# Products of ones into bank 0 where the planned order leaves TensorE without filler, in a recurrent-attention and mixture-of-experts kernel

## Chip, cores and metric

One core of one Trainium2 chip. The metric is device microseconds of one execution; the figure for a kernel is the median of its runs. The profile is one further execution under the hardware profiler.

## What is computed

Three stages. The first is a recurrence over 768 time steps with a 40 x 40 state for each of 4 x 8 heads; the second weighs eight experts with a gate that is normalized over rows and columns in turn; the third is one wide layer with an ELU.

```
for t in range(S):                              # S = 768, D = 40, 32 heads
    y[:, :, t] = einsum('bhd,bhde->bhe', rt, state)
    Sa = einsum('bhde,bhe->bhd', state, at)
    state = state * wt[:, :, None, :] - outer(Sa, bt) + outer(vt, kt)
x = y as [3072, 320]
P = exp(x @ w_gate - max); eight times: rows, then columns normalized
out = sum over e of P[:, e] * (relu(x @ w1[e]) @ w2[e])      # 8 experts, F = 1024
result = elu(out @ w_in) @ w_out                              # width 2048
```

## The kernel before, in words

**Stages.** The recurrence is turned into block algebra over 12 chunks of 64 steps. One chunk takes, in this order: loads (`load_in`, `load_r`, `load_v`); a scan of the decays and reciprocals (`scan`, `recip0` to `recip2`) on VectorE and ScalarE; products of BK with AW (`gmm`, L672, four groups), transposes of AW and BK (`at_t`, `kb_t`); a trip of l_d through DRAM; an elimination of 31 steps on VectorE (`t_mul`, `t_add`, L720 to L730, on TMP and U); a trip of u_d through DRAM; small 32 x 32 products (`emm`, `t21`) and `pmm` (TT with GS, L774); and then, for four groups in a row, the serial part in which the state is carried on (`rvmm`, `y0mm`, `qsmm`, `ysmm`, `trmm`; their results are masked into RHS, and into STMP, ST and Y, by VectorE). `y_out`, `x_in` and `xsplit` turn a chunk's output into the operand XS of the experts; `gatemm` makes its logits.

**Fillers.** Experts 0 and 1 work on a chunk as soon as its XS is there. Their products (XS with w, 128 x 128 x 256; hh or hl with w, 128 x 128 x 320) are cut into short items (`moe0_items`, L878; `moe1_items`, L906), which the planner puts wherever TensorE would else be free. Fillers use banks 0 to 3; attention uses banks 4 to 7. Expert 1 has only the first NSTR = 4 of its 8 blocks done here, and only for chunks 0 to 9; its weights pass through a ring, and a weight split (`stream_split`: a ScalarE copy, a GpSimd subtraction and the reload of the staging tile on SP) is an item of its own. For chunk 9 three more weight splits close the list. Items start in their order: each waits for the first step of the one before (L193 to L198).

**The order.** `Order` (L52) records every call of the first stage as tasks with steps, each on one engine, prices each step (`price`, L130), links steps that touch the same data (`link`, L167), and then plays the engines through by those prices (`run`, L209): of the steps that are ready it takes the one that could begin first, within 200 ns the one of the highest rank, and fillers rank lowest. A spare bank is handed out as it comes free. The planned sequence is then issued to the engines (`replay`, L303); every engine works its own queue in that order. The planner ends when all attention steps are placed; fillers that are left, and chunk 11's, follow in a loop (`moe0_rest`, L1070), in which the gate's normalization is interleaved. After that come all six token blocks for the rest of expert 1, experts 2 to 7 and the last layer (`p2_m1`, `p2_m2`, L1152 to L1184), with TensorE work back to back.

A matmul with both operands in fp32 is recorded as two instructions, one with fp32r operands as one. So the 32 products of one chunk's BK with AW are 64 records, and eight of TT with GS are 16.

Of the kernel before, what the change touches and what calls it, by code (L numbers as in the profile page):

```python
# [9 lines left out]
F32 = mybir.dt.float32  # L10
F32R = mybir.dt.float32r
# [4 lines left out]
ALU = mybir.AluOpType  # L16
# [4 lines left out]
NE, NSETS, NF = 8, 10, 8  # L21
# [1 line left out]
NC = S // C  # L23
NG = 4
NSLOT = 11
NSTR = 4
BIG_X = float(2.0**40)
BIG_W = float(2.0**56)
TINY = float(2.0**-60)
# [16 lines left out]

class Task:
    def __init__(self, f, args, rank=0.0):
        self.f, self.args, self.steps, self.bank, self.rank = f, args, [], None, rank


class Order:  # L52
# [34 lines left out]
    def add(self, f, *args):  # L87
        t = Task(f, args, 1e3 * AHEAD.get(f.__name__, 0))
        self.record(t)
        if t.steps:  # L90
            self.tasks.append(t)
        return bool(t.steps)

    def region(self, ap):

# [113 lines left out]
    def run(self, until=None):  # L209

        self.until = until
        self.link()
        free = dict.fromkeys(("PE", "V", "A", "P", "SP"), 0.0)
        transfers = 0.0
        banks = [0.0] * len(self.banks)
        ready = {e: [] for e in free}
        owed = sum(s.task.f is not until for s in self.steps)

        def open_(s):
            s.left = -1  # L220
            ready[s.eng].append(s)

        for s in self.steps:
            s.left, s.at = len(s.before), 0.0
        for s in self.steps:
            if s.left == 0:
                open_(s)

        def may(s):
            if not s.task.banked or s.task.bank is not None:  # L230
                return True
            return all(p.left == -2 or p.task is s.task for x in s.task.steps for p in x.before)

        done, mode = [], None

        def worth(s):
            return s.rank + (1e3 * self.SAME if s.eng == "PE" and self.tiles(s) == mode else 0.0)

        while owed:
            best = None  # L240
            for e, waiting in ready.items():
                for s in waiting:
                    at = max(free[e], s.at)
                    if e == "SP":
                        at = max(at, transfers - self.QUEUE)
                    if s.task.banked and s.task.bank is None:
                        if not may(s):
                            continue
                        at = max(at, min(banks))
                    key = (at, -s.rank)  # L250
                    if best is None or key < best[0]:
                        best = (key, s)
            at, s = best[0][0], best[1]

            for x in ready[s.eng]:
                begin = max(free[s.eng], x.at)
                if x.eng == "SP":
                    begin = max(begin, transfers - self.QUEUE)
                if x.task.banked and x.task.bank is None:
                    if not may(x):  # L260
                        continue
                    begin = max(begin, min(banks))
                if begin <= at + self.SLACK and worth(x) > worth(s):
                    s = x
            begin = max(free[s.eng], s.at, transfers - self.QUEUE if s.eng == "SP" else 0)
            if s.task.banked and s.task.bank is None:
                b = min(range(len(banks)), key=lambda i: banks[i])
                begin = max(begin, banks[b])
                banks[b] = 1e12
                old = s.task.steps  # L270
                s.task.bank = b
                self.record(s.task)
                for x, y in zip(old, s.task.steps):
                    x.calls = y.calls
                s.task.steps = old
            ready[s.eng].remove(s)
            end = begin + s.cost
            if s.eng == "PE":
                m = self.tiles(s)
                end += 110 * (mode is not None and m != mode)  # L280
                mode = m
            free[s.eng] = end
            result = end + s.tail
            if s.eng == "SP":
                move = s.tail - self.DMA
                transfers = max(transfers, end) + move
                result = transfers + self.DMA
            s.left, s.begin = -2, begin
            done.append(s)
            owed -= s.task.f is not until  # L290
            if s.task.banked and s is s.task.steps[-1]:
                banks[s.task.bank] = result
            for n in s.after:
                n.left -= 1
                n.at = max(n.at, end + 20 * (s.eng != "PE") if n.eng == s.eng != "SP" else result + 40)
                if n.left == 0:
                    open_(n)
        self.done = done
        begun = {s.task for s in done}
        self.replay(done + [s for t in self.tasks for s in t.steps if t in begun and s.left != -2])  # L300
        return [t for t in self.tasks if t not in begun]
# [4 lines left out]
                getattr(self.engines[s.eng], method)(*args, **kwargs)  # L306

    SLACK, QUEUE, FILL, FED, SAME = 200.0, 1000.0, 0.0, 2000.0, 0.0

    @staticmethod  # L310
    def tiles(s):
# [176 lines left out]
def kernel(  # L488
# [64 lines left out]
        wload(i + len(wst))  # L553

    def stream_load(k):
        if k < 10 * NSTR:
            SP.dma_start(out=wst[k % 2], in_=wslab[NF + k % NSTR])

    def stream_split(k):
        if k < 10 * NSTR:
            st, w = wst[k % 2], wring[NF + k % 3]
            A.copy(out=w[:, 0, :], in_=st)
            P.tensor_tensor(out=w[:, 1, :], in0=st, in1=fv(w[:, 0, :]), op=ALU.subtract)
            stream_load(k + 2)
# [339 lines left out]
    def moe1_items(c):  # L906
        x = XS[c % 2]
        if c == 0:
            for k in range(2):
                stream_load(k)  # L910
            for k in range(3):
                stream_split(k)
                yield
        for f in range(NSTR + 1):
            k = c * NSTR + f
            if f < NSTR:
                for half in range(2):
                    mm1(bank[f % 2][:, 0:256], wring[NF + k % 3], x, 4 * half, 4 * half + 4)
                    if half == 1:
                        relu_split(bank[f % 2][:, 0:256], hh[f % 2][:, 0:256], hl[f % 2][:, 0:256])  # L920
                    yield
            if f > 0:
                for t in range(2):
                    cs = slice(128 * t, 128 * t + 128)
                    mm2(bank[2 + t][:, 0:320], hh[(f - 1) % 2][:, cs], hl[(f - 1) % 2][:, cs], wring[NF + (k - 1) % 3],
                        f == 1, f == NSTR)
                    if t == 1 and f == NSTR:
                        for tt in range(2):
                            A.copy(out=YE[:, tt, :], in_=bank[2 + tt][:, 0:320])
                        SP.dma_start(out=ye_d[1][2 * c:2 * c + 2].rearrange("n p d -> p n d"), in_=YE)  # L930
                    yield
                if k + 2 < 10 * NSTR:
                    stream_split(k + 2)
                    yield
        if c == 9:
            wlimit[0] = NSETS * NF - 1
            wload(NF + 1)
            for n in range(NF, NSLOT):
                wsplit(n)
                yield  # L940
# [9 lines left out]
    for c in range(NC):  # L950
# [33 lines left out]
            order.add(f, c)  # L984
        if c < NC - 1:
            stream = chain(moe0_items(c), moe1_items(c) if c < 10 else ())
            while order.add(item):
                pass

    manual = ctx.enter_context(ExitStack())  # L990
    manual.enter_context(tc.manual_schedule())
# [18 lines left out]
    P.memset(Y, 0.0)  # L1010
    V.memset(bank[4], 0.0)

    left = order.run(item)
    ph1.close()

# [5 lines left out]
    OUT = [p2.tile([128, 4, 320], F32, name=f"OUT{j}") for j in range(6)]  # L1021
    RAW = p2.tile([128, 352, 2], I32, name="RAW")
    EX = [p2.tile([128, 512], F32, name=f"EX{i}") for i in range(2)]
    NX = [p2.tile([128, 512], F32, name=f"NSTR{i}") for i in range(2)]
    GX = [p2.tile([128, 512], F32, name=f"GX{i}") for i in range(2)]

    hookq = deque()
# [78 lines left out]
    def evac(s, j):  # L1106
        for t in range(4):
            ps, o, n = bank[2 + t][:, 0:320], OUT[j][:, t, :], 4 * j + t
            if s == 1:
                V.tensor_scalar(out=o, in0=ps, scalar1=pp[:, n, 1:2], scalar2=None, op0=ALU.mult)  # L1110
            elif s < 8:
                V.scalar_tensor_tensor(out=o, in0=ps, scalar=pp[:, n, s:s + 1], in1=o, op0=ALU.mult, op1=ALU.add)  # L1112
            elif s == 8:
# [31 lines left out]

        return [c0, c1]

    first = lambda s, j: NSTR if s == 1 and j < 5 else 0
    units = [(1, j, f) for j in FIRST for f in range(first(1, j), NF)]
    units += [(s, j, f) for s in range(2, NSETS) for j in range(6) for f in range(NF)]  # L1150

# [19 lines left out]
    def p2_m2(i):  # L1171
# [6 lines left out]
        if f == 7:  # L1178
            evac(s, j)
            if s == 7:  # L1180
                for kt in range(3):
                    hookq.append((10, lambda kt=kt: xt2(j, kt)))
        if j == (4 if s == 1 and f >= NSTR else 5):
            late.append(lambda: post_m2(s, f))  # L1184

    LAG = 3
# [102 lines left out]
```

## Time and profile before

| | us |
|---|---|
| median of 3 runs | 2342.08 |
| lowest and highest run | 2340.38, 2345.02 |
| the profiled execution | 2344.47 |
| its span, first to last instruction | 2342.8 |
| outside the span | 1.7 |
| TensorE busy | 2217.4 (95%) |
| VectorE busy | 1235.3 (53%) |
| ScalarE busy | 900.8 (38%) |
| mean granted TensorE clock | 0.953 |

TensorE's clock is granted at one of two levels, 2.4 GHz (1.00) or 1.2 GHz (0.50); a value between is a mean over a stretch. Idle time of an engine is put down to what ended it. Time under "busy" of TensorE is that of modelled, pipelined matmuls: at half clock the same work shows as more busy time.

### The profile page before, as it was taken

The numbers are of one execution on the slowest core, as the hardware profiler recorded it, in microseconds if no ns is written. First come the engines' busy times: TensorE is split into PE (matmuls) and PEld (weight loads), VectorE is DVE, ScalarE is ACT, GpSimd is POOL, SyncE is SP. The second block draws the span as 40 slices with busy tenths as digits, with TensorE's granted clock in tenths as the row PEclk, the third lists the DMA queues.
The fourth block names the chain that finished last, engine by engine and source line by source line (L and its number), as shares of the span: only waits on it lengthen the run. The fifth ranks groups of instructions, "written<-read, shape, count | busy, mean of one in ns | idle before, by whom it ended". The sixth has DMA issues, their size and how long they took to land.

```text
span 2342.8 us, 41612 instructions
## 1 busy us (share of the span) xinstructions
PE 2217.4 (95%) x17276; PEld 1999.4 (85%) x17276; DVE 1235.3 (53%) x2494; ACT 900.8 (38%) x1865; POOL 306.1 (13%) x319
## 2 busy tenths in 40 slices
PE   3888899999999899999999999999999999999997
PEld 3777788888888889999999999999999998999996
DVE  7775478777776363555555442222222333556664
ACT  3454455555555321112112112112112224777664
POOL 2121222222221220002002002002002002001000
PEclk9776899989999899999999999999999999999998
DMA  3443444444443360213222101001001001000000
GB/s 99 100 120 89 107 127 118 134 118 125 113 117 109 98 192 19 78 60 97 76 65 78 48 23 50 1 1 50 1 1 50 1 1 50 1 1 20 19 24 28
DMA packets 171397, 152.60 MB, mean 65 GB/s; under 512 B 107648, under 2 KB 142336, under 8 KB 170240
## 3 DMA queue, kind: packets, MB, share of 16 engines
q1 hardware_dynamic: 171200, 149.86, 23.0%
q8 instruction: 138, 2.26, 0.4%
q14 instruction: 59, 0.48, 0.1%
HBM read 114.83 MB, written 35.00 MB: 64 GB/s over the span
## 4 chain that ended last, share of the span: by engine, by line
PE 86%; DVE 9%; issue 2%; ACT 1%; DMA 1%; SPq 0%; POOL 0%; DVEq 0%; ACTq 0%
PE bank L573 32%; PE bank L306 23%; PE bank L583 10%; PE bank L582 10%; PE bank L581 10%; DVE TMP L306 2%; DVE U L306 2%; DVE RHS L306 1%; DMA wst<-in_wslab_dram 1%; DVE STMP L306 0%; DVE Y L306 0%; DVE ST L306 0%; PE bank L1098 0%; SPq L306 0%; ACT GS L306 0%
## 5 line engine op out<-in xcount | busy, mean ns | idle before, releaser
L573 PE MATMUL bank<-X,w 128*128 128x512 f32 x3296 | 827.6, 392 | 0.0
L573 PEld LDWEIGHTS bank<-X,w 128*128 128x128 f32 x3296 | 601.1, 188 | 105.5
L577 DVE SCALAR_TENSOR_TENSOR hl<-bank,hh 128x512 fp32r<-128x512 f32 x320 | 220.4, 690 | 606.9 <-ACT hh L576 606.9
L583 PE MATMUL bank<-w,hl 128*128 128x320 f32 x1664 | 514.9, 309 | 0.3 <-DVE hl L1092 0.3
L582 PE MATMUL bank<-w,hh 128*128 128x320 f32 x1664 | 514.3, 309 | 0.0
L581 PE MATMUL bank<-w,hh 128*128 128x320 f32 x1664 | 513.7, 309 | 0.0
L576 ACT ACTIVATE hh<-bank 128x512 fp32r<-128x512 f32 x320 | 191.7, 599 | 813.7 <-PE bank L573 812.1
L581 PEld LDWEIGHTS bank<-w,hh 128*128 128x128 f32 x1664 | 313.2, 188 | 16.0
L582 PEld LDWEIGHTS bank<-w,hh 128*128 128x128 f32 x1664 | 313.1, 188 | 15.9
L583 PEld LDWEIGHTS bank<-w,hl 128*128 128x128 f32 x1664 | 313.0, 188 | 0.5 <-DVE hl L1092 0.5
L552 POOL TENSOR_TENSOR w<-wst,w 128x704 fp32r<-128x704 f32 x69 | 118.5, 1719 | 1245.2 <-ACT w L551 1234.0
L306 PE MATMUL bank<-XS,w 128*128 128x256 f32 x1024 | 161.7, 306 | 0.0
L306 PEld LDWEIGHTS bank<-XS,w 128*128 128x128 f32 x1024 | 142.8, 207 | 6.7 <-issue 3.3
L306 DVE TENSOR_TENSOR TMP<-U,LD 128x126 f32<-128x126 f32 (+22 forms) x372 | 135.0, 363 | 13.3 <-DMA LD<-l_d 1.9
L325 DVE SCALAR_TENSOR_TENSOR NSTR<-EX,NSTR 128x512 f32<-128x512 f32 x96 | 67.4, 702 | 135.5 <-ACT NSTR L324 135.2
L306 PE MATMUL bank<-w,hh 128*128 128x320 f32 x512 | 129.5, 340 | 0.1
L306 DVE TENSOR_TENSOR U<-U,TMP 128x126 f32<-128x126 f32 (+22 forms) x372 | 110.4, 297 | 11.4
L1112 DVE SCALAR_TENSOR_TENSOR OUT<-bank,pp,OUT 128x320 f32<-128x320 f32 x144 | 69.3, 544 | 54.1 <-PE bank L583 54.1
L306 POOL TENSOR_TENSOR w<-wst,w 128x704 fp32r<-128x704 f32 x43 | 73.9, 1722 | 175.5 <-ACT w L306 95.0
L306 PE MATMUL bank<-BK,AW 40*64 40x128 f32 x768 | 63.3, 333 | 32.0 <-issue 24.7
L306 DVE SCALAR_TENSOR_TENSOR hl<-bank,hh 128x512 fp32r<-128x512 f32 (+1 forms) x84 | 47.1, 561 | 87.0 <-ACT hh L306 86.6
L306 PEld LDWEIGHTS bank<-w,hh 128*128 128x128 f32 x512 | 87.5, 201 | 4.9 <-issue 1.9
(133 smaller groups left out, 2444.7 us busy)
## 6 DMA issues: line engine op xcount, KB each, us to landing
wst<-in_wslab_dram SPq DMA_DIRECT2D x104, 352.0 KB
RAW<-in_wslab_dram SPq DMA_DIRECT2D x32, 352.0 KB
BK<-in_wakb_dram SPq DMA_DIRECT2D x24, 320.0 KB
x_d<-XS SPq DMA_DIRECT2D x12, 640.0 KB
X<-x_d SPq DMA_DIRECT2D x12, 640.0 KB
ye_d<-YE SPq DMA_DIRECT2D x22, 320.0 KB
XS<-ye_d SPq DMA_DIRECT2D x11, 640.0 KB
LD<-l_d SPq DMA_DIRECT2D x24, 256.0 KB
```

Of the source, the lines that this page charges most:

```text
L306: getattr(self.engines[s.eng], method)(*args, **kwargs)
L325: nc.vector.scalar_tensor_tensor(out=n, in0=e, scalar=1.0, in1=n, op0=ALU.add, op1=ALU.mult)
L552: (V if i < NF else P).tensor_tensor(out=w[:, 1, :], in0=st, in1=fv(w[:, 0, :]), op=ALU.subtract)
L573: PE.matmul(ps, w[:, pl, c0:c0 + 128], x[:, m, :], start=(t == 0), stop=(t == 7))
L576: A.activation(out=h_hi, in_=ps, func=AF.Relu)
L577: V.scalar_tensor_tensor(out=h_lo, in0=ps, scalar=0.0, in1=fv(h_hi), op0=ALU.max, op1=ALU.subtract)
L581: PE.matmul(acc, h_hi, hi, start=first, stop=False)
L582: PE.matmul(acc, h_hi, lo, start=False, stop=False)
L583: PE.matmul(acc, h_lo, hi, start=False, stop=last)
L1112: V.scalar_tensor_tensor(out=o, in0=ps, scalar=pp[:, n, s:s + 1], in1=o, op0=ALU.mult, op1=ALU.add)
```

## The change

The planner keeps a running account of how much of TensorE's array the planned products have used in the last 3.4 us of planned time (`heat`, `activity`). When a TensorE step is placed and would leave TensorE free before it, and no started filler has unplanned steps, and the next filler in line is the first of a chunk (`head`) or there is none, then products of the constant `ones` with itself into bank 0, columns 0 to 127, are put in front of it, at 220 ns each, as long as the account stands below 2600. The count of blocks of expert 1 becomes a list per token block, and three places follow that list. One tile gets another name.

```diff
-NSTR = 4
+STREAM = [4, 4, 4, 4, 4]
+PASSES = [f for c in range(10) for f in range(STREAM[c // 2])]
...
+    def filler(self, f):
+        t = Task(f, ())
+        self.record(t)
+        self.warm = t.steps[0]
+        self.warm.left = -2
...
-        done, mode = [], None
+        done, mode, heat = [], None, deque()
+        fills, pending = deque(t for t in self.tasks if t.f is until), 0
+
+        def cool(t):
+            while heat and heat[0][0] < t - self.WINDOW:
+                heat.popleft()
+            return sum(x for _, x in heat) < self.ACTIVE
...
             ready[s.eng].remove(s)
+            if s.task.f is until and s is s.task.steps[0]:
+                fills.popleft()
+                pending += len(s.task.steps)
+
+            if s.eng == "PE" and not pending and (not fills or fills[0].head):
+                t = free["PE"]
+                while t + 220 <= begin:
+                    if cool(t):
+                        w = Step(self.warm.task, "PE")
+                        w.calls, w.begin, w.cost, w.left = self.warm.calls, t, 220.0, -2
+                        done.append(w)
+                        heat.append((t, 512))
+                        free["PE"] = t + 220
+                    t += 220
+            pending -= s.task.f is until
             end = begin + s.cost
             if s.eng == "PE":
+                heat.append((begin, self.activity(s)))
                 m = self.tiles(s)
...
+    WINDOW, ACTIVE = 3400.0, 2600
+
+    def activity(self, s):
+        cycles = 0
+        for method, args, kwargs in s.calls:
+            out, lhs = args[0], args[1]
+            n = 1
+            for k in out.shape[1:]:
+                n *= k
+            m = lhs.shape[-1]
+            cycles += n * lhs.shape[0] * m / 16384 * (1 if lhs.dtype == F32R else 2 if method == "transpose" else 4)
+        return cycles
...
-            SP.dma_start(out=wst[k % 2], in_=wslab[NF + k % NSTR])
+            SP.dma_start(out=wst[k % 2], in_=wslab[NF + PASSES[k]])
...
+            first = len(order.tasks)
             while order.add(item):
                 pass
+            order.tasks[first].head = True
...
+    def warm():
+        PE.matmul(bank[0][:, 0:128], ones, ones, start=True, stop=True)
+
+    order.filler(warm)
     left = order.run(item)
...
-            if s == 1:
-                V.tensor_scalar(out=o, in0=ps, scalar1=pp[:, n, 1:2], scalar2=None, op0=ALU.mult)
+            if s == 1 or (s == 2 and first(1, j) == NF):
+                V.tensor_scalar(out=o, in0=ps, scalar1=pp[:, n, s:s + 1], scalar2=None, op0=ALU.mult)
...
-    first = lambda s, j: NSTR if s == 1 and j < 5 else 0
+    first = lambda s, j: STREAM[j] if s == 1 and j < 5 else 0
```

## Rows read from the trace of the kernel before

**Rows 1.** The page: span, clock by 40 slices, and shares of the chain.
```profile
span 2342.8 us, 41612 instructions
...
PE   3888899999999899999999999999999999999997
...
PEclk9776899989999899999999999999999999999998
...
PE 86%; DVE 9%; issue 2%; ACT 1%; DMA 1%; SPq 0%; POOL 0%; DVEq 0%; ACTq 0%
```

**Rows 2.** Stretches: busy us (instructions) of PE, PEld, DVE, ACT, POOL; clock; DMA share, GB/s.
```profile
57.00:80.00 23.00, 17.62 (x228) 16.35 (x230) 13.99 (x18) 11.33 (x27) 5.95 (x8) 1.00 0.56 131
80.00:86.80 6.80, 6.04 (x110) 5.15 (x106) 5.71 (x20) 4.61 (x12) 1.08 (x2) 1.00 0.23 59
86.80:131.00 44.20, 39.76 (x412) 33.78 (x414) 31.44 (x76) 18.25 (x55) 9.43 (x14) 0.50 0.42 97
...
155.00:203.00 48.00, 45.40 (x444) 40.53 (x445) 30.59 (x59) 22.60 (x60) 9.04 (x12) 0.50 0.44 109
177.00:203.00 26.00, 26.00 (x264) 24.15 (x263) 11.25 (x17) 12.68 (x33) 3.88 (x8) 0.50 0.35 96
```

**Rows 3.** TensorE's timeline: start, length, products; first one, and BK with AW.
```profile
10.68 2.78 PE L306 MATMUL bank<-ident,AW 40*64 40x40 f32 x48 [10.68 <-DVE AW L306]
...
17.32 7.09 PE L306 MATMUL bank<-BK,AW 40*64 40x128 f32 x64 [2.34 <-issue]
...
178.70 3.68 PE L306 MATMUL bank<-BK,AW 40*64 40x128 f32 x32
...
332.92 1.96 PE L306 MATMUL bank<-BK,AW 40*64 40x128 f32 x32
```

**Rows 4.** TensorE's timeline around 80 us: TT with GS before and after.
```profile
75.37 3.71 PE L306 MATMUL bank<-TT,GS 128*104 128x128 f32 x16 [1.30 <-issue]
...
80.32 2.00 PE L306 MATMUL bank<-TT,GS 128*104 128x128 f32 x16
```

**Rows 5.** Timelines of TensorE and SP: the first filler, and the end of chunk 9's.
```profile
127.91 2.93 PE L306 MATMUL bank<-XS,w 128*128 128x256 f32 x12
...
782.77 1.08 PE L306 MATMUL bank<-R,SN 40*40 40x64 f32 x16 [1.13 <-DVE Y L306]
...
791.33 0.78 SPq L306 DMA_DIRECT2D wst<-in_wslab_dram  x1
```

**Rows 6.** GpSimd's timeline at the start.
```profile
3.92 0.21 POOL L1002 MEMSET ones<- 128x128 f32 x1
```

**Rows 7.** VectorE's timeline: chunk 0's elimination, first and last of 62, and what follows.
```profile
36.63 0.21 DVE L306 TENSOR_TENSOR TMP<-U,LD 128x31 f32<-128x31 f32 x1 [1.86 <-DMA LD<-l_d]
...
56.19 0.19 DVE L306 TENSOR_TENSOR U<-U,TMP 128x16 f32<-128x16 f32 x1
56.30 2.50 DVE L306 TENSOR_TENSOR BK<-BK,A 104x512 f32<-104x512 f32 x4
```

**Rows 8.** Waits, total, times, longest: VectorE 80 to 116 us; TensorE 80 to 128.
```profile
DVE RHS L306 <- PE bank L306: 5.3, 3, 3.5
DVE STMP L306 <- PE bank L306: 1.4, 3, 0.8
...
PE bank L306 <- DVE RHS L306: 1.5, 2, 0.7
PE bank L306 <- DVE Y L306: 1.1, 1, 1.1
```

**Rows 9.** The chain in order of time: start, length, what.
```profile
113.54 7.11 PE bank L306 x64
...
163.49 48.77 PE bank L306 x548
```

**Rows 10.** Timelines of TensorE and VectorE at the end of chunk 7's fillers.
```profile
671.36 2.23 PE L306 MATMUL bank<-RHS,KB 128*40 128x104 f32 x16 [4.41 <-DVE RHS L306]
...
667.56 0.28 DVE L306 TENSOR_TENSOR U<-U,TMP 128x120 f32<-128x120 f32 x1
...
668.31 1.65 DVE L306 TENSOR_TENSOR U<-U,TMP 128x133 f32<-128x133 f32 x1
```

More of the change, by code (lines that the diff above doesn't have):

```diff
@@ L48, in __init__ @@
     def __init__(self, f, args, rank=0.0):
-        self.f, self.args, self.steps, self.bank, self.rank = f, args, [], None, rank
+        self.f, self.args, self.steps, self.bank, self.rank, self.head = f, args, [], None, rank, False
 class Order:
@@ L557, in stream_load @@
     def stream_load(k):
-        if k < 10 * NSTR:
-            SP.dma_start(out=wst[k % 2], in_=wslab[NF + k % NSTR])
+        if k < len(PASSES):
+            SP.dma_start(out=wst[k % 2], in_=wslab[NF + PASSES[k]])
     def stream_split(k):
-        if k < 10 * NSTR:
+        if k < len(PASSES):
             st, w = wst[k % 2], wring[NF + k % 3]
@@ L913, in moe1_items @@
                 yield
-        for f in range(NSTR + 1):
-            k = c * NSTR + f
-            if f < NSTR:
+        n = STREAM[c // 2]
+        for f in range(n + 1):
+            k = sum(STREAM[i // 2] for i in range(c)) + f
+            if f < n:
                 for half in range(2):
@@ L925, in moe1_items @@
                     mm2(bank[2 + t][:, 0:320], hh[(f - 1) % 2][:, cs], hl[(f - 1) % 2][:, cs], wring[NF + (k - 1) % 3],
-                        f == 1, f == NSTR)
-                    if t == 1 and f == NSTR:
+                        f == 1, f == n)
+                    if t == 1 and f == n:
                         for tt in range(2):
@@ L931, in moe1_items @@
                     yield
-                if k + 2 < 10 * NSTR:
+                if k + 2 < len(PASSES):
                     stream_split(k + 2)
@@ L1023 @@
     EX = [p2.tile([128, 512], F32, name=f"EX{i}") for i in range(2)]
-    NX = [p2.tile([128, 512], F32, name=f"NSTR{i}") for i in range(2)]
+    NX = [p2.tile([128, 512], F32, name=f"NX{i}") for i in range(2)]
     GX = [p2.tile([128, 512], F32, name=f"GX{i}") for i in range(2)]
@@ L1182, in p2_m2 @@
                     hookq.append((10, lambda kt=kt: xt2(j, kt)))
-        if j == (4 if s == 1 and f >= NSTR else 5):
+        if j == (4 if s == 1 and f >= STREAM[4] else 5):
             late.append(lambda: post_m2(s, f))
```

## Prediction

> **What bounds the kernel now.** I read the page first, then the engines by stretches, then TensorE's timeline and the chain of waits. From about 840 us on TensorE is full at full clock and nothing of the change reaches there; all the room is in the first third, where the slices of TensorE and of its clock dip [rows 1]. The chain gives TensorE 86% and VectorE 9% of the span [rows 1], so time taken out of a stretch in which TensorE ends last does reach the end.
>
> The clock comes next. The reader is to see that TensorE is busy 39.76 us between 86.8 and 131 and 45.40 us between 155 and 203, all at half clock [rows 2]. The 1.00 that the windows show before 80 us is not a measurement: the 64 products of BK and AW at 17.32 took 7.09 us, 111 ns each, and 32 of them in a stretch recorded at 0.50 took 3.68 us, 115 ns each, against 61 ns (1.96 us for 32) at full clock [rows 3]. So TensorE runs at 1.2 GHz, half its rate, until the clock rises at 80 us behind products that use nearly the whole array [rows 2, 4]. It falls again at 86.8 us though TensorE was busy 6.04 of 6.80 us before, with small products [rows 2].
>
> **What the change does, and what it doesn't.** STREAM holds 4 five times, so PASSES, the counts and every `first` are the old numbers; the new branch in evac needs a first of 8 and never fires. The rest is a renamed tile. What remains is the product of ones by ones, 128x128, into bank 0. Its place is found after `begin` of the next TensorE step is fixed, and it fills only up to `begin`; `free` is overwritten right after. So the planner's order of all other instructions, with every DMA and queue, is the old one, and the only new thing is products standing in front of TensorE instructions.
>
> It asks two things: that no step of a filler already begun is still unplanned, and that the next filler is the first of its chunk. In chunk 0 that holds from the start to the first real filler, which ran at 127.91 us [rows 5]. At later chunk ends the last filler is a weight split, whose copy, subtraction and reload must be planned first, and by then the next chunk's fillers are mostly there. At the very end chunk 9's last reload was issued at 791.33 us, behind the attention's last waits such as that at 782.77 [rows 5], so I expect no products of ones there. The cold stretch of 155 to 203 us lies inside chunk 0's fillers and gets none either.
>
> **Price of one.** The nearest rows are the eight fp32 products of a 104-column weight with 128 columns (16 records): 3.71 us at half clock, 0.46 us each, and 2.00 us at full, 0.25 us each [rows 4]. The planner gives 220 ns and places about six per 3.5 us (512 each, until 2600 are in its window of 3.4 us). Bank 0 is read by nobody while they run, since all filler steps are planned by then, so they wait only for the memset of ones at 3.92 us [rows 6].
>
> **Part by part, against the profiled 2344.5 us.**
>
> *Start, 0 to 24 us.* I estimate 18 products before the first attention product (10.68 us [rows 3]), three bursts of six. Running from 4.1 us, all at half clock, they take 18 x 0.46 = 8.3 us and end at 12.4, 1.7 us late; if the clock rises midway they end in time. Then the 64 products of BK and AW take 64 x 61 = 3.9 instead of 7.09 us. What follows on the path is the copy, the trip of l_d through DRAM and VectorE's elimination. Bounds: +1.7 (clock never rises) to -3.2. I take -3.2, since the nearest row at which the clock rose stands behind 3.71 us of just such wide products [rows 4].
>
> *The gap, 35 to 57 us.* TensorE does nothing while VectorE eliminates from 36.63 to 56.38 us and then multiplies BK [rows 7]. The planner spaces its bursts over this gap, some 36 products; the chip cannot: an in-order engine runs them as soon as it reaches them. They are done in 36 x 0.25 = 9 us (17 at half clock), below 22 in either case, so nothing is late; but the clock has every time to fall before 57 us. Gain 0.
>
> *57 to 80 us.* The products of 57 us run at half rate as before. Further products of ones go into gaps of together 23.00 - 17.62 = 5.4 us [rows 2]. About nine of them cost 4.1 us at half clock; if badly placed they delay the path, if they raise the clock at 75 instead of 80 us they save 3.71 - 2.00 = 1.7 us [rows 4]. I take 0, bounds -3 and +4.
>
> *80 to 113 us.* If the clock stays up, TensorE halves its work, but VectorE interleaves chunk 1's elimination here and is the next late one: what it waited for TensorE after 80.5 us is 1.8 us for RHS (5.3 less the 3.5 before 80.51) and 1.4 for STMP [rows 8]. That 3.2 is the ceiling; I take -2.5. The cover that hides the products of ones is this waiting for VectorE.
>
> *113 to 131 us.* The 64 products of 113.54 stand alone on the chain with 7.11 us [rows 9]; at 61 ns they take 3.9: -3.2. The first fillers then start at full clock and not after 3.1 us (127.9 to 131) of half: -1.6. Together -4.8, bounds -6 and 0.
>
> *Later.* TensorE waits 4.41 us before 671.36 with chunk 7's fillers gone, and the clock then falls. But the gap is long because VectorE's additions there took 1.65 us instead of some 0.28 [rows 10], which the planner does not price, and its window is full from the fillers just before. I count 0, bounds -3 and +1 for products of ones that stand in front of work that is ready.
>
> Sum: -3.2 + 0 + 0 - 2.5 - 4.8 + 0 = -10.5 us, 2334.0 for the profiled execution. That ran 2.4 us above the median of 2342.1, so I predict **2332**. All later stages follow unchanged but earlier, since their loads wait for buffers that come free earlier too.
>
> **Rivals.**
>
> *A second cold stretch shortened.* After 131 us the same order runs some 10 us earlier, and the clock's rise at 203 us may fall elsewhere: what stands together there is a mixture of fillers and small products, and 177 to 203 us is 26.00 of 26.00 us busy at half clock with VectorE at 11.25 [rows 2]. At full clock that is 13 us less, on a piece of 48.77 us that the chain gives to TensorE alone [rows 9]; I count 12. Then 2320. Against it: no product of ones goes there, and a later rise is as possible in itself.
>
> *No effect.* The products run in a clump at the front of each wait, the clock falls behind them, and the real products find it as before: 2337 to 2347. For it speaks the gap of 35 to 57 us. The Trainium skill ("TensorE: Matmul & The Clock Gate", section "Why this matters for your kernels") asks for no long idle gap between bursts of matmuls, since idle time throttles the clock, and makes no difference of what the bursts hold; by that only the gap at 35 would matter and the change would give nothing. The trace disagrees with it: from 86.8 to 128 us TensorE's longest wait for one row was 1.1 us [rows 8] and the clock was at half all the time. What else would make it void is that products of ones do not count as work for the clock; no row shows whether they do.
>
> *Slower.* The place is 57 to 113 us and the mechanism products of ones at half clock in front of real ones. If the clock does not rise, some 40 of them at 0.46 us are 18.4 us, against idle time of 5.4 us in 57 to 80, 0.8 in 80 to 86.8 and 4.4 in 86.8 to 131, 10.6 in all [rows 2]: about +8, 2350. It decides if the additional work fails to lift the clock by 80 us, where it rose without help.
>
> **Chances.** Forecast 0.42, second stretch 0.20, no effect 0.22, slower 0.16. A measurement tells about 0.2%, 4.7 us, from no change. Of the forecast's own range (2326 to 2340, its bounds) a little falls inside that: faster 0.60, same 0.24, slower 0.16. The range runs from 2316, which holds the second stretch, to 2347, which holds no effect; outside lie the slower case and the far ends.
>
> **What the changed profile would show.** Right: TensorE busy from 4 us on; the 64 products at 17 us in about 4 us, and those before 57 us in a clump with an idle tail; granted clock 1.00 from 80 us to 155; the 64 products of 113 us in 4 us; the first fillers about 10 us earlier; no new products past 128 us but a handful. Wrong: a granted clock of 0.50 between 87 and 128 us; real products after 57 us waiting behind products of ones; more than some 200 of these in all; or a cold stretch after 155 us longer than 48 us, which would eat the gain.

## The result and the profile after

The changed kernel takes 2323.32 us (median of 6 runs, 2316.40 to 2329.96), the kernel before 2343.36 in the 6 runs beside it (2340.38 to 2345.02): a ratio of 0.9917, interval 0.9895 to 0.9938. The profiled execution took 2321.35 us. A second set of four runs gave 2327.51 against 2341.35 (0.9932, 0.9905 to 0.9959). The forecast was 2332, the range 2316 to 2347.

The page of the changed kernel: span, TensorE and its granted clock in 40 slices, chain. The lines answer to [rows 1].

```profile
span 2319.6 us, 42104 instructions
...
PE   6897999999999899999999999999999999999997
...
PEclk8977999999999899999999999999999999999998
...
PE 85%; DVE 9%; issue 2%; ACT 1%; DMA 1%; POOL 0%; SPq 0%; DVEq 0%; ACTq 0%
```

TensorE has 17522 matmul records instead of 17276, so 123 products of ones at two records each, and all of them stand before the first real filler. TensorE's timeline of the changed kernel shows the largest groups and what they led to (columns as in [rows 3]):

```profile
4.17 6.71 PE L336 MATMUL bank<-ones 128*128 128x128 f32 x36 [4.17 <-POOL ones L1048]
10.81 1.59 PE L336 MATMUL bank<-ident,AW 40*64 40x40 f32 x48
...
17.20 3.71 PE L336 MATMUL bank<-BK,AW 40*64 40x128 f32 x64 [1.45 <-issue]
...
29.47 11.05 PE L336 MATMUL bank<-ones 128*128 128x128 f32 x82
54.08 6.24 PE L336 MATMUL bank<-BK,AW 40*64 40x128 f32 x56 [13.56 <-issue]
...
63.44 1.97 PE L336 MATMUL bank<-ones 128*128 128x128 f32 x14
...
71.03 1.97 PE L336 MATMUL bank<-TT,GS 128*104 128x128 f32 x16 [0.21 <-issue]
...
75.72 0.92 PE L336 MATMUL bank<-RHS,KB 128*40 128x104 f32 x16
...
104.30 3.71 PE L336 MATMUL bank<-BK,AW 40*64 40x128 f32 x64 [1.20 <-ACT RHS L336]
...
114.86 1.69 PE L336 MATMUL bank<-XS,w 128*128 128x256 f32 x12
```

The reader is to see three things. Chunk 0's 64 records of BK with AW (32 products, which the prediction calls 64) take 3.71 us instead of the 7.09 of [rows 3], and those of chunk 2 3.71 instead of 7.11 [rows 9]. The 41 products of ones in the long wait are over 13.56 us before it ends, and the records of BK with AW behind them (56 of the 64 lie in this view's window) take 111 ns each, half rate. And the first filler starts at 114.86 us, not 127.91 [rows 5].

The windows of both kernels between the same instructions (busy us of TensorE, clock, DMA share, GB/s) say where the rest of the time went. The cuts are at chunk 1's BK with AW, the first KB product, chunk 2's BK with AW, the first filler, chunk 1's first filler, chunk 10's first filler, the end. Before:

```profile
57.10:82.30 25.20, 19.91 (x250) 1.00 0.51 120
82.30:113.50 31.20, 26.92 (x329) 0.57 0.30 75
113.50:127.90 14.40, 13.48 (x148) 0.50 0.57 112
127.90:259.70 131.80, 111.04 (x1223) 0.69 0.38 103
259.70:789.40 529.70, 496.20 (x6511) 0.93 0.44 117
789.40:2342.80 1553.40, 1529.44 (x8569) 0.99 0.14 41
```

After:

```profile
54.10:75.70 21.60, 20.94 (x284) 0.77 0.60 140
75.70:104.30 28.60, 24.32 (x370) 0.94 0.30 83
104.30:114.90 10.60, 9.72 (x167) 1.00 0.66 128
114.90:233.80 118.90, 98.90 (x1222) 0.77 0.43 116
233.80:763.10 529.30, 492.57 (x6511) 0.94 0.44 117
763.10:2319.60 1556.50, 1531.05 (x8569) 0.99 0.14 41
```

The start gave 3.0 us (57.1 to 54.1), the next three stretches 3.6, 2.6 and 3.8: 13.0 by the first filler. The fourth stretch, which holds no product of ones, gave another 12.9. The fifth gave 0.4, and the last lost 3.1. Together 23.2, the difference of the spans. (The 1.00 in the first window of before is again the stretch without a record.) These are one execution of each kernel; the second pair, under `s_same` and `s_base`, is needed to see which of these differences come every time.

### The profile page after: what moved, and what is told of

It reads as the page before. It is cut to its first block, busy times and chain, and to the rows that moved or that the text cites. A ratio compares the mean times of both kernels' runs of the same rounds, so it can differ in the third digit from the quotient of the medians.

```text
span 2319.6 us, 42104 instructions
## 1 busy us (share of the span) xinstructions
PE 2211.1 (95%) x17522; PEld 1994.6 (86%) x17522; DVE 1238.6 (53%) x2494; ACT 899.4 (39%) x1865; POOL 309.6 (13%) x319
## 4 chain that ended last, share of the span: by engine, by line
PE 85%; DVE 9%; issue 2%; ACT 1%; DMA 1%; POOL 0%; SPq 0%; DVEq 0%; ACTq 0%
PE bank L616 32%; PE bank L336 22%; PE bank L626 10%; PE bank L625 10%; PE bank L624 10%; DVE TMP L336 2%; DVE U L336 2%; DVE RHS L336 1%; DVE Y L336 0%; DVE STMP L336 0%; DVE ST L336 0%; DMA wst<-in_wslab_dram 0%; PE bank L1148 0%; DVE A L336 0%; ACT A L336 0%
## 5 line engine op out<-in xcount | busy, mean ns | idle before, releaser
L336 DVE TENSOR_TENSOR TMP<-U,LD 128x126 f32<-128x126 f32 (+22 forms) x372 | 135.0, 363 | 14.3 <-DMA LD<-l_d 2.8
L369 DVE SCALAR_TENSOR_TENSOR NX<-EX,NX 128x512 f32<-128x512 f32 x96 | 67.4, 702 | 135.5 <-ACT NX L368 135.2
L1162 DVE SCALAR_TENSOR_TENSOR OUT<-bank,pp,OUT 128x320 f32<-128x320 f32 x144 | 69.3, 544 | 54.1 <-PE bank L626 54.1
L366 ACT ACTIVATE NX<-bank 128x512 f32<-128x512 f32 x96 | 57.4, 598 | 84.4 <-PE bank L616 84.4
```

Source lines behind the costliest of these rows:

```text
L366: nc.scalar.activation(out=n, in_=h, func=AF.Relu, scale=-1.0)
L369: nc.vector.scalar_tensor_tensor(out=n, in0=e, scalar=1.0, in1=n, op0=ALU.add, op1=ALU.mult)
```

## Experiments

My theory: the clock rises and stays up by how much of TensorE's array is in use, each group of products acts on the stretch it stands in, and the 12.9 us after the first filler are a matter of where the clock's next rise falls.

**Only the products before the long wait.** The same insertion, with a count (in this and the next kernels `placed` numbers the products as the planner places them):

```diff
+                        self.placed += 1
+                        if self.placed <= 35:
                             done.append(w)
```

> Only the first 35 products of ones stay, those in front of the long wait; the 41 in the wait and the 47 behind it go. Theory (every piece acts on the stretch it stands in): BK with AW of chunk 0 takes 3.7 us instead of 7.1, chunk 1's BK with AW starts some 3 us earlier (54 us), and from there the clock is at half until about 77 us and again from about 84 to 128, so the first filler starts near 125 us: about -3 us by the first filler. What follows up to 260 us depends on where the clock's changes fall, so 2340 if the second cold stretch stays at 48 us, 2328 if it is shortened. Rival (the warm start is what keeps the clock up later too): first filler near 115 us, 2323.

2338.94 against 2341.19 (0.9989, 0.9975 to 1.0003, so not told from no change). Chunk 1's products started at 54.9, the first filler at 124.5 as expected, and the two stretches behind the wait ran at half clock as before, but for some 10 us from 76.5 us on (6.8 from 80.0 in the kernel before):

```profile
54.90:109.90 55.00, 45.09 (x576) 0.59 0.39 98
109.90:124.50 14.60, 13.51 (x149) 0.50 0.56 110
124.50:256.20 131.70, 110.97 (x1221) 0.69 0.38 103
```

The rival, that a warm start carries on by itself, falls.

**Only the products behind the long wait.** `if self.placed > 76:`

> Only the last 47 products stay, those behind the long wait (57 to 113 us in the kernel before). Theory: start as before the change, BK with AW of chunk 0 at 111 ns each; the clock rises near 67 us instead of 80, no long cold stretch up to 128 us, the first filler about 10 us earlier than before (118 us). About -10 at the first filler and 2333, or 2321 if the second cold stretch is shortened too. Rival (the start carries the gain): first filler at 125 us or later, 2340.

2332.08 (0.9951, 0.9934 to 0.9967), first filler at 116.8. Chunk 1's products began at 56.3 us; the first window starts where the clock rose, at 66.4:

```profile
66.40:106.50 40.10, 35.40 (x574) 0.96 0.45 115
106.50:116.80 10.30, 9.70 (x167) 1.00 0.71 133
116.80:241.60 124.80, 105.09 (x1223) 0.74 0.41 110
```

So these 47 alone bring the first filler 11.1 us forward (127.9 to 116.8), the 35 at the start alone 3.4, and all together 13.0.

**Without the 41 in the long wait.** `if not 35 < self.placed <= 76:`

> The 41 products in the long wait of 35 to 57 us go, the other 82 stay. Theory (they stand at the front of the wait and the clock has fallen again when it ends): chunk 1's BK with AW at 54 us and at half clock as with the change as made, first filler at 115 us, 2323 within 5. Rival (they are what brings the later stretch to full clock): first filler some us later, 2330.

2328.30 (0.9938, 0.9916 to 0.9960) with the first filler at 115.4 us and chunk 1's products at 54.6 at half rate, as with the change as made, which took 2327.51 in the runs beside it (`s_same` below). A third of the added products are worth nothing that these runs show, as the prediction said.

**Filling the long wait to its end.** 50 more behind the last of the 41: `if self.placed == 76: done += [w] * 50`.

> 50 further products of ones behind the 41 in the long wait, 91 in all, at 0.27 us each about 24.6 us: they last until chunk 1's BK with AW is due at 54 us. Theory: the clock is at 1.00 through the wait, the 64 products of BK with AW take 3.8 instead of 6.2 and more us, and the first filler starts 2 to 3 us earlier than with the change as made (112 us); 2320, less or more by what the later cold stretches do. Rival (products in the wait are worth nothing however many, since what follows waits for VectorE): first filler at 115 us; or they overrun the wait and it starts later.

2330.11 (0.9952, 0.9935 to 0.9970), first filler at 115.1. This run did not test what it was for. At full clock one product took 0.226 us in such a clump, not 0.27, so they were over at 49.79 us and 4.27 us were left, in which the clock fell:

```profile
29.20 20.59 PE L340 MATMUL bank<-ones 128*128 128x128 f32 x182
54.06 7.09 PE L340 MATMUL bank<-BK,AW 40*64 40x128 f32 x64 [4.27 <-issue]
```

A later kernel (`s_hand0` below) has 101 there; TensorE then had no wait, and the 64 products took 3.71 us:

```profile
32.23 22.82 PE L339 MATMUL bank<-ones 128*128 128x128 f32 x202
54.98 3.71 PE L339 MATMUL bank<-BK,AW 40*64 40x128 f32 x64
```

From there to chunk 2's products it took 47.4 us instead of 50.2 (54.1 to 104.3). But the first filler stood at 117.8 in that run, since the clock fell at 104.5 us:

```profile
102.40:117.80 15.40, 15.36 (x166) 0.57 0.70 150
```

And in `s_hand`, which has the same 101, the 64 records also took 3.71 us, but the clock fell at 62.3 us, behind the next wait (2.27 us), and the stretch took 51.2 us. What filling the long wait to its end is worth stays open; an earlier first filler by 2 to 3 us was not seen.

**The same products on a corner of the array.**

```diff
-        PE.matmul(bank[0][:, 0:128], ones, ones, start=True, stop=True)
+        PE.matmul(bank[0][0:32, 0:128], ones[0:32, 0:32], ones[0:32, :], start=True, stop=True)
```

> The same 123 products at the same places, but of a 32x32 corner of ones with 128 columns, so TensorE is as busy and uses a sixteenth of the array. Theory (how much of the array is used lifts the clock): half clock up to about 80 us and from 87 to 131 as in the kernel before; the products, now at half clock, add little; first filler at 126 to 130 us, 2338 to 2350. Rival (being busy without gaps keeps the clock up, whatever is multiplied): the clock and the time of the change as made, first filler at 115 us, 2323.

2353.14 us, slower than before (1.0043, 1.0026 to 1.0060), just past the expected end. The products are as many and keep TensorE as occupied, but the clock does not rise in the waits of 60 to 80 us, and they stand in front of work that is ready:

```profile
40.14 17.70 PE L336 MATMUL bank<-ones 32*32 32x128 f32 x82
60.36 7.09 PE L336 MATMUL bank<-BK,AW 40*64 40x128 f32 x64 [2.53 <-issue]
...
84.06 1.99 PE L336 MATMUL bank<-TT,GS 128*104 128x128 f32 x16
...
118.10 7.09 PE L336 MATMUL bank<-BK,AW 40*64 40x128 f32 x64
```

Chunk 1's products begin 3.3 us later than before the change, the first filler at 135.2 us, 7.3 later. The clock rose at 82.9 us, behind the first TT with GS as in the kernel before, and fell at 103.4. So occupying TensorE did not bring the rise forward; the size of the products did: the rise came at 64 to 68 us in all seven profiles in which chunk 1's BK with AW ran at half rate and the 18 full-size products stood behind it. On holding the clock this run says less: it stayed up for 20.5 us, in the kernels without products from 78 us on for 6.8 to 17.1, and with the change as made from 63.9 to 139 us but for 3.4.

**Only the first 18 behind the wait.** `if self.placed <= 94:` (the 76 before them stay)

> Of the 47 products of ones behind the long wait only the first 18 stay (those between 60 and 71 us of the changed kernel); the 29 in the waits for VectorE from 78 us on go. Theory (each keeps the clock up only where it stands): the clock rises near 64 us as with the change as made, falls again between 80 and 92 us and stays at half to about 113; the first filler at 119 to 121 us, between the 115 of the change as made and the 125 without all 47. Rival (once risen, the clock keeps itself up): the first filler at 115 us.

2336.24 (0.9971, 0.9955 to 0.9988), first filler at 121.9, 0.9 past the expected end. From chunk 1's products to chunk 2's 52.0 us, between the 55.0 of `s_start` and the 50.2 of the change as made; then 14.3 at half clock and not 10.6:

```profile
55.60:107.60 52.00, 47.47 (x614) 0.66 0.41 103
107.60:121.90 14.30, 13.43 (x148) 0.50 0.54 111
```

So of the 47, the 18 in the waits of 60 to 71 us bring 3.0 us and the 29 from 78 us on 1.8 and then 3.7, in one execution each. The clock, once up, did not keep itself up: it rose at 66.3 us and fell at 83.4.

**The change as made, and the kernel before, once more.**

> The change as made, once more, for the spread of its second cold stretch between executions. Theory (the length of the half-clock stretches after 128 us changes between executions, since the clock's changes fall at other places each time): first filler at 115 us again, but another sum of half-clock time between 128 and 260 us than the 58 us of the first profile. Rival (it follows from the order alone): the same stretches within 4 us.

> The kernel before, once more, for the same question. Theory: the clock's changes fall at other places, so the cold stretch of 155 to 203 us has another length or place, and the time moves with it. Rival (fixed by the order): 48 us again within 4, and 2343 within 3.

The changed kernel: 2327.51, the profiled execution 2329.03. The first filler stood at 115.7 again, but the stretch from it to chunk 1's first filler took 130.4 us at a mean clock of 0.70, not 118.9 at 0.77:

```profile
105.50:115.70 10.20, 9.67 (x166) 1.00 0.72 132
115.70:246.10 130.40, 109.76 (x1225) 0.70 0.40 106
```

Its cold stretch lasted from 142 to 189 us, where the first profile had 139 to 163. The kernel before took 2341.95 (profiled execution 2337.24), its first filler stood at 126.6, and its stretch took 127.3 us (131.8 in the first profile) with the rise at 189 instead of 203. The order is the same in each pair, so the order does not fix the time: where the clock rises differs from execution to execution. That part of the theory stands, and 11.5 us of the first profile's gain do not come every time. In this second pair the change gives 10.9 us by the first filler and its stretch behind it is 3.1 us longer than without the change.

**Ten products inside that cold stretch.** In front of chunk 2's first product of R with SN:

```diff
+    def spot():
+        PE.matmul(bank[4][0:96, 416:512], ones[:, 0:96], ones[:, 0:96], start=False, stop=False, skip_group_check=True)
...
+            if s.eng == "PE":
+                done += [self.spot] * self.AHEAD_OF.pop((s.task.f.__name__, *s.task.args), 0)
...
+    AHEAD_OF = {('y0mm', 2, 0): 10}
```

> The change as made, and ten 96x96 products of ones (columns 416 to 511 of bank 4, adding to what stands there, which nothing reads) in front of chunk 2's first product of R with SN, at about 151 us, inside the cold stretch that begins at 139 to 142 us. Theory (that stretch lasts to 163 us in some executions and to 189 in others because little is missing for the rise): it now ends by 160 us in every execution, the stretch from the first filler to chunk 1's first filler takes 115 to 120 us, never 130, and the median is 2316 to 2322 with little spread. Rival (its length has another cause): runs up to 2330 as before, all some 2 to 3 us later for the ten products at half clock.

2326.19 (2321.38 to 2327.76; 0.9931, 0.9911 to 0.9951). The clock did rise, at 160.5 us, right behind the ten (3.51 us at half clock), and the products behind them ran at full rate:

```profile
155.84 1.12 PE L338 MATMUL bank<-R,VE 40*64 40x64 f32 x16
156.89 3.51 PE L338 MATMUL bank<-ones 128*96 128x96 f32 x20
160.33 0.72 PE L338 MATMUL bank<-R,SN 40*40 40x64 f32 x16
```

But it fell again at 171 and 184 us, the stretch took 125.5 and not 115 to 120, and in this execution there was a cold stretch ahead of the first filler as well (119.3). The median did not move against the 2327.5 and 2323.3 of the change as made and missed the 2316 to 2322; four runs do not show whether the spread got smaller. That ten products can bring the rise is seen once; that they shorten the stretch is not. This cold stretch ahead of the first filler (105.9 to 123.0 us) and that of `s_hand0` are two in the eight profiles that have all 47 full-size products behind the wait: there it took 15.4 us from chunk 2's products to the first filler, in the other six 10.1 to 10.6. So the first filler stood at 114.1 to 119.3 with them, and at 124.5 to 127.9 in the three profiles with no products behind the wait.

**Everywhere the plan has TensorE waiting.** The two conditions dropped (`if s.eng == "PE":`), with 96x96 products at 165 ns and 288. They open a new sum in bank 4 while the attention's y sums are open there, so those come out different; instructions and sizes are as said.

> Products of ones wherever the plan leaves TensorE waiting, with filler in line or without: 96x96, into columns 416 to 511 of bank 4, which nothing reads, priced 165 ns and 288. Theory (the cold stretches inside the fillers, 139 to 163, 194 to 207 and 218 to 238 us of the changed kernel, are lost to the same cause): these get shorter, the clock stays up through most of 128 to 260 us, and the time falls by another 5 to 12 us to 2311 to 2318. Rival (there the real order has other gaps than the plan, and the products stand in front of work that is ready): no gain or a loss of up to 5 us, 2323 to 2328.

2336.02 (0.9978, 0.9963 to 0.9992): worse than the rival, but not for the reason that it gave. The clock did stay up longer from filler to filler (0.88), yet the stretch took 120.7, and the next one 538.4 instead of 529.3:

```profile
120.50:241.20 120.70, 101.01 (x1308) 0.88 0.44 115
241.20:779.60 538.40, 502.46 (x6592) 0.93 0.45 115
```

Of the loss, 5.6 us stand before the first filler (120.5 against 114.9), where both conditions hold anyway. What differs there is the product: 96x96 and into bank 4, out of which VectorE and ScalarE read the y sums. Some of these products waited for that reading too, and so stood behind the wait and in front of ready work:

```profile
93.97 0.92 PE L336 MATMUL bank<-ones 128*96 128x96 f32 x8 [1.63 <-DVE Y L336]
94.82 0.65 PE L336 MATMUL bank<-R,SN 40*40 40x64 f32 x16
```

So this run does not show what dropping the two conditions costs, and whether the plan's waits are the chip's where fillers are in line stays open.

**At waits read from the profile.** Nine steps of chunks 1 to 4 that waited in the profile of the changed kernel, and 60 more in the long wait; then 19 further steps up to chunk 11.

```diff
+    AHEAD_OF = {('ysmm', 1, 2): 5, ('y0mm', 1, 3): 6, ('ysmm', 1, 3): 3, ('trmm', 1, 3): 3, ('y0mm', 2, 2): 2,
+                ('qsmm', 2, 2): 3, ('ysmm', 2, 2): 20, ('y0mm', 2, 3): 5, ('gmm', 4, 0): 28}
```

> The change as made, with 60 more products in the long wait of 30 to 54 us and 75 products of 96x96 (bank 4, columns 416 to 511) in front of nine TensorE steps of chunks 1 to 4 that waited 0.5 to 6.4 us in the profile of the changed kernel; each count is about the wait divided by 0.2 us. Theory (products of ones at measured waits hold the clock and delay nothing): hardly any half clock from 30 to 260 us, first filler at 112 to 115 us, from there to chunk 1's first filler 103 to 112 us and not 119 or 130; 2305 to 2314. Rival (what follows those waits is bound by VectorE, so a full clock there is worth little): 116 us or more for that stretch, 2317 or later.

> As the one before, with 91 more products in front of 19 further steps of chunks 3 to 11 that waited 0.5 to 4.4 us. Theory: most of the 62 us of half clock between chunk 1's first filler and chunk 10's go too, and the short one at the end of the first stage; another 5 to 15 us, 2293 to 2307. Rival (the short cold stretches there stand in full TensorE work of small products, not behind waits, so filling waits does not reach them): within 3 us of the one before.

The first took 2317.38, but with runs of 2315.87 to 2338.00 (0.9913, 0.9883 to 0.9943); its profile fell on the slowest, in which the clock fell at 145 us in spite of the products. The second took 2311.68 (2310.90 to 2321.98): 0.9888, 0.9860 to 0.9916, the lowest median of all these kernels, below the kernel before and below the change as made, though these last two were not timed side by side. Its windows:

```profile
104.00:114.10 10.10, 9.69 (x166) 1.00 0.69 132
114.10:231.80 117.70, 106.65 (x1375) 0.88 0.43 115
231.80:756.50 524.70, 494.19 (x6703) 0.98 0.44 119
```

Both missed the forecasts (2305 to 2314 and 2293 to 2307); the second is 5.7 us below the first, where 5 to 15 were expected. At a clock of 0.88 the second stretch still took 117.7 us, 1.2 less than at 0.77. The rival says that VectorE bounds it, but these runs do not show that either. The products write bank 4, and part of them did not stand in the wait that they were meant for:

```profile
140.83 2.24 PE L339 MATMUL bank<-ones 128*96 128x96 f32 x12 [1.60 <-DVE Y L339]
142.99 1.08 PE L339 MATMUL bank<-R,SN 40*40 40x64 f32 x16
```

They waited for VectorE's Y as the product of R with SN does, and then held that product up by 2.2 us. All four waits for Y in this stretch (4.9 us) stand in front of such products. Whether products of ones that do run in those waits would gain anything was not tested.

## Why the prediction held, point by point

- **The order and the places** were read rightly: no product of ones behind the first filler, and every old instruction in the old order.
- **Start, -3.2:** measured -3.0. The opening products (18, as estimated) took 6.71 us, the clock rose at 9.28 us, and the first attention product started at 10.81 us instead of 10.68 [rows 3]. `s_start` has 3.4 for the first filler.
- **The long wait, 0:** 41 products where 36 were estimated, over by 40.52, the clock down again at 43.4; `s_nogap` shows no worth of theirs.
- **57 to 80 us, taken as 0, bounds -3 and +4:** this term was mis-sized. From chunk 1's BK with AW to the first KB product it took 21.6 us instead of 25.2, so -3.6, past the end that I had kept. The products in the waits raised the clock at 63.9 us, 16 us earlier than before, and not at 75 as I had allowed: `emm` ran at full rate, and so did the first group of TT with GS (1.97 us against the 3.71 of [rows 4]; the second ran at full rate before, too). `s_mid` sets 3.0 us against these 18 products.
- **80 to 113 us, -2.5 under a ceiling of 3.2:** measured -2.6. VectorE's waits for TensorE there, 1.8 and 1.4 us in [rows 8], are down to 0.3 and 0.2:

```profile
DVE RHS L336 <- PE bank L336: 0.3, 1, 0.3
DVE STMP L336 <- PE bank L336: 0.2, 1, 0.2
```

- **113 to 131 us, -3.2 and -1.6:** -3.8 up to the first filler, but +1.0 in the two executions (`s_rise`, `s_hand0`) in which the clock fell there; the 1.6 behind it cannot be read apart from the next stretch.
- **Sum:** -8.9 up to the first filler was forecast (10.5 less that 1.6), -13.0 came, 3.6 of the difference from the one term.
- **The likeliest case was not the one that came in the first profile.** The rival of the shorter cold stretch was: 12 us were counted for it, 12.9 measured, its 2320 against 2321.35. No product of ones stands there, and the rise came at 163 instead of 203 us. What I had not seen is that this differs between executions. `s_same` has the long form, 130.4 us, so that the rival came true in that one profile by luck. The median of 2323.32 lies between forecast and rival, 8.7 us below the forecast: outside the forecast's own 2326 to 2340, and inside the whole range because that was drawn to hold the rival.
- **The signs.** The clock was not at 1.00 from 80 to 155 us: it was at 0.50 from 91.2 to 94.6, which was named as a sign of being wrong, and again from 139. The other signs named as right came.
- **Slower** by products at half clock in front of ready work did not happen, because the clock rose. `s_small` shows that mechanism at 2353, where 2350 was worked out.
- **No effect** falls with `s_late` and `s_mid`: products in short waits bring the first filler forward. The Trainium skill ("TensorE: Matmul & The Clock Gate", section "Why this matters for your kernels") asks for no long idle gaps between bursts of matmuls. The runs agree where TensorE did stand idle (4.27 us in `s_longgap`, and the clock fell), but before the change the clock was at half from 86.8 to 128 us with no wait above 1.1 us [rows 8], which that rule does not tell.
- **Not foreseen:** the last stage lost 3.1 us (1556.5 against 1553.4). The clock fell there one time more than before, at 825 us, where TensorE waits for the normalization on VectorE, 6.7 us in all instead of 5.1. In `s_same` that stage took 1554.7, so this too differs between executions; I did not test it.

## What to carry to other kernels

Ask of each stretch at half clock what the engine did before it fell, and not only whether it waited: here products on a corner of the array did not bring the rise forward, and full-size ones in the short waits did (64 to 68 us; 77 to 80 without products there, 83 with the corner). Products put into a long wait were run at its front, and the clock fell again before its end. Look where such products write, too: here some of those into a bank that VectorE still read waited for it (1.6 us) and then stood in front of ready work. And before a gain is put down to an edit, look at a second execution for stretches that the edit does not touch.

## What was not expected

With the instruction order unchanged, the stretch from the first filler to chunk 1's first filler took 118.9 and 130.4 us in two executions of the changed kernel, and 131.8 and 127.3 in two of the kernel before. The changed kernel's runs spread over 13.6 us (2316.40 to 2329.96), those of the kernel before, beside it, over 4.6; but 19 later runs of the kernel before spread over 12.1 (2334.20 to 2346.33), so the change is not shown to widen the spread. Ten products (3.5 us of TensorE at half clock) were followed by a rise, and 48 us of mixed work before the change, TensorE busy for 45.40 of them [rows 2], had not brought it until their end. What decides it in one execution and not in the next was not settled.
